# Attention and a feed-forward block in one kernel: the weights' place in SBUF, modulo 256 bytes, against the activations'

## The chip, the cores and the metric

The kernel runs on one core of a Trainium2 chip. The metric is the device time of one execution in microseconds. Before the change three runs took 956.99, 957.62 and 958.03 us; the median is 957.62.

## What is computed

Attention output of eight batches and eight heads (a downsampled full attention plus a local one within three positions), laid out as 4608 tokens of 512 values, goes through a feed-forward block:

```python
out_d = sm_attn(q_d, k_d, v_d)            # on means over 4 positions
out_up = np.repeat(out_d, factor, axis=2)
mask = np.abs(pos[:, None] - pos[None, :]) < factor
out_local = np.matmul(attn, v)            # softmax of the masked scores
x = (out_up + out_local)                  # (B, H, S, D) -> (4608, 512)
h = x @ w_in                              # 512 -> 2048
r = np.maximum(h, 0.0)
g = s * (r * r) + b
return g @ w_out                          # 2048 -> 512
```

Each float32 operand of the feed-forward block is split into a high and a low part of type float32r, and a product is three matmuls: high by high, high by low, low by high.

## The kernel before

The 4608 tokens are 18 blocks `t` of 256, the 2048 columns of the hidden layer are eight pairs `p` of two 128-column tiles (the "f pairs"). For each block and pair there is

- a first GEMM (`products1`, L617): 24 matmuls of 256 columns. The stationary operand is a 128x128 piece of `wi[p]`, the moving one a 128x256 piece of `xh` or `xl`. A block and pair's 24 matmuls are called a run here. There are 18 x 8 = 144 runs, 3,456 matmuls;
- on ACT relu, square and the cast to `gh` (`upper`, L630 to L632), on DVE the remainder `gl` (`lower`, L637);
- a second GEMM (`products2`, L691 to L693): 12 matmuls of 512 columns, 1,728 in all. Here a 128x128 piece of `gh` or `gl` is stationary and `wo[p]` is the moving operand.

While one matmul streams its moving operand, the next one's stationary operand is loaded; the page lists these loads as PEld.

Blocks 0 and 1 go through pairs 0 to 6 together while the weights arrive, then block 2, then block after block with pairs 0 to 7. Attention of later batches runs on DVE, POOL and ACT beside the GEMMs up to about 720 us; its own matmuls stand between those of the GEMMs. A plan written by hand (`PLAN`) fixes the order of the start on every engine, and a scheduler orders the rest by priorities.

Memory is laid out pool by pool in the order in which pools are opened, a tile after the other within a pool. Sizes are rounded up to 32 bytes a partition. Nearly all of it is in use: the last buffer ends at 229,320 bytes of a partition. The pools that matter here:

- `cst`: constants, the strip mask among them (L159, 384 bytes, read only at the start by L176 and L177), `eps`, `sb_s`, `sb_b` with one value each
- `one`: tiles with one buffer. `wi` and `wo` of all eight pairs stand in it (8,192 bytes each: 2 parts x 4 x 256 or 2 x 2 x 512 values), the tags `os` and `xl2` (4,096 bytes each), and attention's tiles. Tags `wi0` to `wo7` are also lent out before the weights arrive: as staging of raw weights (`load_w`, L227) and as room for the first batch's attention (`make_room`, L113)
- `two`: tiles with two buffers, among them `xh`, `xl`, `gh`, `gl`, and `pv`, which serves the weight conversion (`convert`, L240) and later local attention

Block 2's parts of x are kept in `os` and `xl2`. From block 3 on every third pair (`p % 3 == 2`, that is 2 and 5) has its g in `xl2`, under the name `gb`.

By the built program's memory map, the start addresses modulo 256 before the change are:

| tiles | modulo 256 |
|---|---|
| wi, wo of pairs 0 and 1 | 224 |
| wi, wo of pairs 2 to 7 | 96 |
| xh, xl, gh, gl | 32 |
| os, xl2 (block 2's x, and gb) | 96 |

The pieces inside a tile that a matmul takes lie multiples of 512 bytes apart, so each matmul has the distance of its two tiles. The functions that the change touches:

Of the kernel before, what the change touches and what calls it, by code (L numbers as in the profile page):

```python
# [11 lines left out]
F32 = mybir.dt.float32  # L12
F32R = mybir.dt.float32r
I32 = mybir.dt.int32
# [5 lines left out]
P = 128  # L20
# [4 lines left out]
DM = H * D  # L25
# [13 lines left out]
NFP = DFF // 256  # L39
NK = DM // P  # L40
# [9 lines left out]
STAGE = (7, 6, 7, 6, 7, 6, 7)  # L50
# [36 lines left out]
def attention_ffn_kernel(ctx, tc, qk, vw_in, vr_in, vdm, qkn, vn, w_in, w_out, s_in, b_in, out):  # L87
    nc = tc.nc
    PS = bass.MemoryType.PSUM

    cst = ctx.enter_context(tc.tile_pool(name="cst", bufs=1))
    one = ctx.enter_context(tc.tile_pool(name="one", bufs=1))
    two = ctx.enter_context(tc.tile_pool(name="two", bufs=2))
    ps = ctx.enter_context(tc.tile_pool(name="ps", bufs=1, space=PS))
# [7 lines left out]
    def take(flat, at, shape):  # L102

        v = flat[0 : shape[0], at : at + math.prod(shape[1:])]
        return v.rearrange("p (a c) -> p a c", a=shape[1]) if len(shape) == 3 else v


    def flat(tag, n, pool=one):
        return pool.tile([P, n], F32, tag=tag, name="flat")
# [1 line left out]
    room = {}  # L111

    def make_room(i):  # L113
        sc, dg = flat(f"wi{6 - i}", 2048), flat(f"wo{6 - i}", 2048)
        if i == 1:
            big = flat("x", HP * S, two)
            lp = {"vw": take(big, 0, [P, NG, P]), "vd": take(big, 768, [KM, FAC, P])}
            pl, at = big, 1280
        else:
            big = flat("wi2" if i == 2 else "wo2", 2048)  # L120
            pl, at = flat("os" if i == 2 else "xl2", 1024), 512
            lp = {"qk": take(big, 0, [P, 2, SP]), "vw": take(big, 2 * SP, [P, NG, P]),
                  "vd": take(pl, 0, [KM, FAC, P])}
        lp["vr"] = take(sc, 1792, [P, FAC, D])
        return {"sc": sc, "dg": dg, "load": lp, "pl": take(pl, at, [P, 2 * NG, 32]),
                "sm": take(pl, at + 384, [P, 2, 2 * NG])}

    def load_parts(b, hp, parts):
        if b == 0 and hp and hp not in room:
            room[hp] = make_room(hp)  # L130
        own = room[hp]["load"] if b == 0 and hp else {}
        got = ld.setdefault((b, hp), {})
        for tag in parts:
            shape, src, pool = {
                "qk": ([P, 2, SP], qk[b, hp], two),
                "vr": ([P, FAC, D], vr_in[b, hp], one),
                "vd": ([KM, FAC, P], vdm[b, hp], one),
                "vw": ([P, NG, P], vw_in[min(HP * b + hp, EU - 1)], one)}[tag]
            t = own[tag] if tag in own else pool.tile(shape, F32, tag=tag, name="t" + tag)
            nc.sync.dma_start(t, src)  # L140
            got[tag] = t
# [14 lines left out]

    mask = cst.tile([P, 3, 32], F32, name="mask")  # L159
    nc.gpsimd.memset(mask, 0.0)  # L160

    def keep(ap, pattern, base, cm):
# [31 lines left out]
    ones = cst.tile([P, P], F32, name="ones")  # L194
    nc.gpsimd.memset(ones, 1.0)
    bias = cst.tile([P, DM], F32, name="bias")
    eps = cst.tile([P, 1], F32, name="eps")
    nc.gpsimd.memset(eps, 4e-9)

    db = one.tile([P, 2 * NG, P], F32, tag="big", name="db")  # L200
# [21 lines left out]
    wi, wo, wst = {}, {}, {}  # L222
# [4 lines left out]
    def load_w(p, op):  # L227
        if op == "i":
            src = src_i[:, :, 512 * p : 512 * p + 512]
        else:  # L230
            src = src_o[:, 2 * p : 2 * p + 2]
        if p < len(STAGE):
            st = one.tile([P, 1024, 2], I32, tag=f"w{op}{STAGE[p]}", name="wst")
        else:
            st = new_x(2).rearrange("p h s -> p (h s)")[:, 0:2048].bitcast(I32)
            st = st.rearrange("p (f t) -> p f t", t=2)
        nc.sync.dma_start(st.rearrange("p (k f) t -> p k (f t)", k=src.shape[1]), src)
        wst[(p, op)] = st

    def convert(st, hi, lo, op, p):  # L240


        n = hi.shape[1]
        top, low = st[:, :, 1], st[:, :, 0]
        if n <= 512:
            f = two.tile([P, n], F32, tag="pv", name="es")
        else:
            f = one.tile([P, n], F32, tag="xl2" if op == "i" else "os", name="es")
        w = f.bitcast(I32)


        nc.scalar.mul(f, top.bitcast(F32), 2.0 ** -112)
        yield
        nc.vector.tensor_scalar(f, f, W_MAX, -W_MAX, ALU.min, ALU.max)
        nc.vector.tensor_scalar(w, w, 3, 0x7FFFFFF8, ALU.logical_shift_left, ALU.bitwise_and)
        yield
        nc.vector.scalar_tensor_tensor(w, low, 29, w, ALU.logical_shift_right, ALU.bitwise_or)  # L257
        nc.vector.scalar_tensor_tensor(w, top, -0x80000000, w, ALU.bitwise_and, ALU.bitwise_or)
        yield
        nc.scalar.copy(hi, f)  # L260
        yield
        nc.vector.tensor_tensor(lo, f, hi.bitcast(F32), ALU.subtract)  # L262

    def split_parts(p):
        wi[p] = one.tile([P, 2, NK, 256], F32R, tag=f"wi{p}", name="wi")
        wo[p] = one.tile([P, 2, 2, DM], F32R, tag=f"wo{p}", name="wo")
        for op, w in (("i", wi[p]), ("o", wo[p])):
            fl = w.rearrange("p s k f -> p s (k f)")
            n = 1024 if WIDE <= p < len(STAGE) else 512
            for j in range(0, 1024, n):  # L270
                js = slice(j, j + n)
                yield convert(wst[p, op][:, js], fl[:, 0, js], fl[:, 1, js], op, p)
# [4 lines left out]
    def new_x(b):  # L277
        if b not in xt:
            xt[b] = two.tile([P, HP, S], F32, tag="x", name="x")
        return xt[b]  # L280
# [494 lines left out]
    for op in "io":  # L775
        load_w(0, op)
    for hp in range(1, HP):
        load_parts(0, hp, ("vw",))
    sb_s = cst.tile([P, 1], F32, name="sb_s")
    nc.sync.dma_start(sb_s, bass.AP(s_in.tensor, s_in.offset, [[0, P], [1, 1]]))  # L780
    sb_b = cst.tile([P, 1], F32, name="sb_b")
    nc.sync.dma_start(sb_b, bass.AP(b_in.tensor, b_in.offset, [[0, P], [1, 1]]))
    for op in "io":
        load_w(1, op)
# [14 lines left out]

    bk = {0: banks(*range(8)), 1: two_banks(5, 6), 2: two_banks(2, 3)}  # L800
    chunks = (chunk for p in range(NFP) for chunk in split_parts(p))

    streams = {"x": begin_x(), "y": third_x(), "z": fourth_x(), "b": add_rows()}
# [15 lines left out]
    def load(name):  # L819
        if name[0] == "w":  # L820
            load_w(int(name[1]), name[2])
        else:
            load_parts(*units[int(name[1:-1])], {"k": ("qk",), "v": ("vr", "vd"), "w": ("vw",)}[name[-1]])
# [75 lines left out]
    for st in range(begin, len(order)):  # L899
        t, p = order[st]  # L900
# [73 lines left out]
```

## Time and profile before

| what | value |
|---|---|
| median of three runs | 957.62 us |
| profiled execution, device time | 957.84 us |
| its span, first to last instruction | 956.0 us |
| TensorE matmuls busy | 928.4 us |
| first GEMM (L617), busy over all 3,456 | 437.00 us |
| mean granted TensorE clock | 0.989 |

Times are microseconds unless marked ns. PE is TensorE's matmuls, PEld its weight loads, DVE is VectorE, ACT ScalarE, POOL GpSimd. A line with "xN | busy, mean ns" is a group of N instructions. Matmuls are pipelined, so the mean length of one matmul's record (280 ns for 256 columns) is longer than the distance between the starts of two neighbours; where a text speaks of spacing, it is the distance between starts. The chain of waits lists in order of time what was last at each moment: a row has the start, the length, and how many instructions in a row it covers.

### The profile page before, as it was taken

How to read it: one execution, taken by the hardware profiler on the slowest of the kernel's cores; microseconds unless marked ns; L12 is line 12 of the kernel's file. 1: busy time of each engine (PE TensorE's matmuls, PEld its weight loads, DVE VectorE, ACT ScalarE, POOL GpSimd, SP SyncE). 2: the span in 40 equal slices, each digit the busy share in tenths (PEclk: the TensorE clock that was granted, in tenths of full speed). 3: DMA queues.
4: the chain of work that ended last, by engine and by line, in shares of the span. 5: the costliest groups of instructions: out<-in, count | busy, mean ns of one | idle time of the engine just before them, and what ended most of it. 6: DMA issues, size and time to landing. Idle time of an engine off the chain costs nothing.

```text
span 956.0 us, 18449 instructions
## 1 busy us (share of the span) xinstructions
PE 928.4 (97%) x7316; PEld 835.7 (87%) x7316; DVE 639.5 (67%) x1134; ACT 476.8 (50%) x1133; POOL 416.2 (44%) x440
## 2 busy tenths in 40 slices
PE   6699999999999999999999999999999999999998
PEld 5588888888898999998899999999899999999986
DVE  8999999845587788787868787887777321112021
ACT  7977774466552636344454544454544333333231
POOL 6401130010577676867776868676776200000000
PEclk9699999999999999999999999999999999999999
DMA  9755413123232323323232323232311000000000
GB/s 322 268 167 183 143 46 118 63 75 100 87 117 89 117 90 110 95 80 108 88 116 80 126 80 126 81 126 79 114 55 44 1 23 2 23 1 23 1 23 22
DMA packets 31750, 86.25 MB, mean 90 GB/s; under 512 B 3248, under 2 KB 7856, under 8 KB 31664
## 3 DMA queue, kind: packets, MB, share of 16 engines
q1 hardware_dynamic: 31664, 85.08, 26.9%
q8 instruction: 57, 0.93, 0.4%
q14 instruction: 29, 0.24, 0.1%
HBM read 75.63 MB, written 9.44 MB: 89 GB/s over the span
## 4 chain that ended last, share of the span: by engine, by line
PE 84%; DVE 7%; DMA 3%; POOL 2%; ACT 1%; issue 1%; SPq 0%; DVEq 0%; POOLq 0%
PE ph L617 38%; PE po L691 13%; PE po L692 13%; PE po L693 12%; PE sa L327 2%; PE ol L464 1%; PE up L368 1%; POOL pr L522 1%; DMA tqk<-in_qk_dram 1%; PE ot L554 1%; DMA wst<-in_moe_w_in_dram 1%; DMA tvd<-in_vdm_dram 1%; PE up L366 1%; PE sl L421 1%; DVE es L257 1%
## 5 line engine op out<-in xcount | busy, mean ns | idle before, releaser
L617 PE MATMUL ph<-xh,wi 128*128 128x256 f32 x2176 | 406.7, 280 | 1.5 <-DVE gl L637 1.5
L617 PEld LDWEIGHTS ph<-xh,wi 128*128 128x128 f32 x2176 | 342.0, 189 | 7.3 <-DVE gl L637 1.9
L617 PE MATMUL ph<-xl,wi 128*128 128x256 f32 x1152 | 323.4, 281 | 0.0
L522 POOL TENSOR_TENSOR pr<-lqk 128x576 f32<-128x576 f32 x140 | 201.3, 1461 | 77.7 <-DMA lqk<-in_qkn_dram 47.7
L617 PEld LDWEIGHTS ph<-xl,wi 128*128 128x128 f32 x1152 | 217.3, 189 | 4.5
L630 ACT ACTIVATE ph<-ph 128x512 f32<-128x512 f32 x144 | 83.7, 582 | 248.1 <-PE ph L617 239.4
L691 PE MATMUL po<-wo,gh 128*128 128x512 f32 x456 | 181.8, 399 | 2.0 <-DVE os L669 1.7
L693 PE MATMUL po<-wo,gl 128*128 128x512 f32 x456 | 179.1, 394 | 1.1 <-DVE gl L637 1.0
L692 PE MATMUL po<-wo,gh 128*128 128x512 f32 x456 | 180.2, 395 | 0.0
L637 DVE TENSOR_TENSOR gl<-ph,gh 128x512 fp32r<-128x512 f32 x114 | 77.9, 684 | 125.0 <-ACT gh L632 124.7
L544 POOL TENSOR_TENSOR acc<-acc,pv 128x576 f32<-128x576 f32 x80 | 121.0, 1512 | 48.8 <-DVE acc L544 25.9
L524 DVE TENSOR_REDUCE st<-pr 128x9 f32<-128x576 f32 x140 | 105.9, 757 | 31.7 <-POOL pr L522 28.2
L693 PEld LDWEIGHTS po<-wo,gl 128*128 128x128 f32 x456 | 85.7, 188 | 20.5 <-DVE gl L637 2.5
L691 PEld LDWEIGHTS po<-wo,gh 128*128 128x128 f32 x456 | 85.7, 188 | 18.7 <-DVE os L669 2.1
L632 ACT CAST gh<-ph 128x512 fp32r<-128x512 f32 x114 | 66.6, 586 | 66.4 <-PE po L692 61.1
L692 PEld LDWEIGHTS po<-wo,gh 128*128 128x128 f32 x456 | 85.8, 188 | 15.7 <-DVE wo L262 0.3
L297 POOL TENSOR_TENSOR dq<-vt 80x64 f32<-80x64 f32 x58 | 22.6, 401 | 174.5 <-PE up L368 172.9
L543 DVE TENSOR_TENSOR pv<-lv,st 128x576 f32<-128x576 f32 x120 | 86.9, 747 | 14.2 <-POOL acc L544 13.6
L631 ACT ACTIVATE ph<-ph 128x512 f32<-128x512 f32 x144 | 83.8, 583 | 3.5
L692 PE MATMUL po<-wo,gb 128*128 128x512 f32 x120 | 47.8, 398 | 0.0
L691 PE MATMUL po<-wo,gb 128*128 128x512 f32 x120 | 47.1, 392 | 0.0
L693 PE MATMUL po<-wo,gb 128*128 128x512 f32 x120 | 46.8, 392 | 0.0
(158 smaller groups left out, 1167.5 us busy)
## 6 DMA issues: line engine op xcount, KB each, us to landing
tqk<-in_qk_dram SPq DMA_DIRECT2D x30, 584.0 KB, 3.9
lqk<-in_qkn_dram SPq DMA_DIRECT2D x20, 768.0 KB, 4.6
lv<-in_vn_dram SPq DMA_DIRECT2D x20, 480.0 KB, 3.4
out_dram<-os SPq DMA_DIRECT2D x17, 512.0 KB, 3.0
wst<-in_moe_w_in_dram SPq DMA_DIRECT2D x7, 1024.0 KB, 6.2
wst<-in_moe_w_out_dram SPq DMA_DIRECT2D x7, 1024.0 KB, 5.0
tvd<-in_vdm_dram SPq DMA_DIRECT2D x29, 160.0 KB, 2.6
tvr<-in_vr_dram SPq DMA_DIRECT2D x29, 128.0 KB, 3.1
```

Source lines behind the costliest of these rows:

```text
L522: nc.gpsimd.tensor_tensor(pr, lqk[:, 0:CH], lqk[:, CH + o : 2 * CH + o], ALU.mult)
L524: nc.vector.tensor_reduce(ls[:, :, o], pr, AX.X, ALU.add)
L543: nc.vector.tensor_tensor(pv, lv[:, o : o + CH], w, ALU.mult)
L544: (nc.vector if o % 3 == 1 else nc.gpsimd).tensor_tensor(acc[:, :, h], acc[:, :, h], pv, ALU.add)
L617: nc.tensor.matmul(ph[:, j], wi[p][:, s, k, f], xk[:, k], start=k == 0 and s == 0 and xk is xh, stop=k == NK - 1 and s == 1)
L630: nc.scalar.activation(ph, ph, AF.Relu)
L631: nc.scalar.activation(ph, ph, AF.Square)
L632: nc.scalar.copy(gh, ph)
L637: nc.vector.tensor_tensor(gl, acc.pop((t, p)), gh.bitcast(F32), ALU.subtract)
L691: nc.tensor.matmul(po[m], gh[:, j, ms], wo[p][:, 0, j], start=first, stop=False)
L692: nc.tensor.matmul(po[m], gh[:, j, ms], wo[p][:, 1, j], start=False, stop=False)
L693: nc.tensor.matmul(po[m], gl[:, j, ms], wo[p][:, 0, j], start=False, stop=last)
```

## The change

The weights of pairs 0-1, 2-3, 4-5 and 6-7 move out of `one` into four pools of their own. Each of the four begins with a gap of 64 bytes; a further pool with a gap of 32 bytes stands behind them. The strip mask moves from `cst` into a buffer of `pv`, and `eps`, `sb_s` and `sb_b` become three columns of one tile; both make room for the gaps.

```diff
     cst = ctx.enter_context(tc.tile_pool(name="cst", bufs=1))
+    weights = []
+    for i in range(NFP // 2):
+        weights.append(ctx.enter_context(tc.tile_pool(name=f"w{i}", bufs=1)))
+        weights[i].tile([P, 16], F32, tag="gap", name="gap")
+    ctx.enter_context(tc.tile_pool(name="gap", bufs=1)).tile([P, 8], F32, name="gap")
+    wpool = lambda tag: weights[int(tag[2]) // 2]
     one = ctx.enter_context(tc.tile_pool(name="one", bufs=1))
...
-        sc, dg = flat(f"wi{6 - i}", 2048), flat(f"wo{6 - i}", 2048)
+        sc, dg = (flat(f"w{op}{6 - i}", 2048, weights[3 - (i + 1) // 2]) for op in "io")
...
-            big = flat("wi2" if i == 2 else "wo2", 2048)
+            big = flat("wi2" if i == 2 else "wo2", 2048, weights[1])
...
-    mask = cst.tile([P, 3, 32], F32, name="mask")
+    mask = two.tile([P, 3, 32], F32, tag="pv", name="mask")
...
-    eps = cst.tile([P, 1], F32, name="eps")
+    small = cst.tile([P, 3], F32, name="small")
+    eps, sb_s, sb_b = (small[:, i : i + 1] for i in range(3))
...
-            st = one.tile([P, 1024, 2], I32, tag=f"w{op}{STAGE[p]}", name="wst")
+            tag = f"w{op}{STAGE[p]}"
+            st = wpool(tag).tile([P, 1024, 2], I32, tag=tag, name="wst")
...
-        wi[p] = one.tile([P, 2, NK, 256], F32R, tag=f"wi{p}", name="wi")
-        wo[p] = one.tile([P, 2, 2, DM], F32R, tag=f"wo{p}", name="wo")
+        wi[p] = wpool(f"wi{p}").tile([P, 2, NK, 256], F32R, tag=f"wi{p}", name="wi")
+        wo[p] = wpool(f"wo{p}").tile([P, 2, 2, DM], F32R, tag=f"wo{p}", name="wo")
...
-    sb_s = cst.tile([P, 1], F32, name="sb_s")
     nc.sync.dma_start(sb_s, bass.AP(s_in.tensor, s_in.offset, [[0, P], [1, 1]]))
-    sb_b = cst.tile([P, 1], F32, name="sb_b")
     nc.sync.dma_start(sb_b, bass.AP(b_in.tensor, b_in.offset, [[0, P], [1, 1]]))
```

By the memory map of the changed program:

| tiles | modulo 256 | weights minus x, first GEMM | g minus weights, second GEMM |
|---|---|---|---|
| wi, wo of pairs 0 and 1 | 224 | 96 | 160 |
| wi, wo of pairs 2 and 3 | 32 | 160 | 96 (pair 2 from gb: 160) |
| wi, wo of pairs 4 and 5 | 96 | 224 | 32 (pair 5 from gb: 96) |
| wi, wo of pairs 6 and 7 | 160 | 32 | 224 |
| xh, xl, gh, gl | 128 | | |
| os, xl2 | 192 | | |

On all five engines the instructions stand in the same order as before, and so do the DMA issues. One wait is new. On ACT, in the start, before (a row's name of several tiles is written as `flat`, the first batch's borrowed room; `es` is the conversion's tile in `pv`):

```order
L342 ACTIVATE pd<-pd,dsm 96x144 x2
L331 ACTIVATE flat<-flat 96x3 [waits DVE_49]
L333 ACTIVATE flat<-sa,flat 96x144 [waits PE_49,Activation_49]
L333 ACTIVATE flat<-sa,flat 96x144 x2
L252 ACTIVATE es<-wst 128x512
L331 ACTIVATE flat<-flat 96x3 [waits DVE_49]
```

And after, where the file's lines stand eight further down (L260 is L252 before):

```order
L350 ACTIVATE pd<-pd,dsm 96x144 x2
L339 ACTIVATE flat<-flat 96x3 [waits DVE_49]
L341 ACTIVATE flat<-sa,flat 96x144 [waits PE_49,Activation_49]
L341 ACTIVATE flat<-sa,flat 96x144 x2
L260 ACTIVATE es<-wst 128x512 [waits Pool_49]
L339 ACTIVATE flat<-flat 96x3 [waits DVE_49]
```

The order is the same; the second conversion step now waits for POOL, which wrote the mask into the buffer that this step takes.

## The prediction

> **What bounds the kernel now.** I read the page first, then the chain of waits for one late output block, the timeline inside single runs, and the groups of windows that hold one weight pair each.
>
> ```profile
> PE 928.4 (97%) x7316; PEld 835.7 (87%) x7316; DVE 639.5 (67%) x1134; ACT 476.8 (50%) x1133; POOL 416.2 (44%) x440
> PEclk9699999999999999999999999999999999999999
> PE 84%; DVE 7%; DMA 3%; POOL 2%; ACT 1%; issue 1%; SPq 0%; DVEq 0%; POOLq 0%
> PE ph L617 38%; PE po L691 13%; PE po L692 13%; PE po L693 12%; PE sa L327 2%; PE ol L464 1%; PE up L368 1%; POOL pr L522 1%; DMA tqk<-in_qk_dram 1%; PE ot L554 1%; DMA wst<-in_moe_w_in_dram 1%; DMA tvd<-in_vdm_dram 1%; PE up L366 1%; PE sl L421 1%; DVE es L257 1%
> L617 PE MATMUL ph<-xh,wi 128*128 128x256 f32 x2176 | 406.7, 280 | 1.5 <-DVE gl L637 1.5
> ```
>
> TensorE is busy 97% of the span at a full granted clock after the start, and 38 + 13 + 13 + 12 = 76% of the chain that ended last is the two GEMMs. So the time is the number of matmuls, which the change leaves alone, times the spacing of two neighbours. That spacing can be read per weight pair. The chain of waits in block 16 (854 to 907 us, no attention left on the other engines) shows the eight runs of 24 first-GEMM matmuls, pairs 0 to 7 in order:
>
> ```profile
> 854.69 2.83 PE ph L617 x24
> 860.28 2.83 PE ph L617 x24
> 868.60 2.75 PE ph L617 x24
> 873.44 2.73 PE ph L617 x24
> 876.86 2.73 PE ph L617 x24
> 883.08 2.74 PE ph L617 x24
> 887.88 2.83 PE ph L617 x24
> 893.47 2.83 PE ph L617 x24
> ```
>
> The runs have the same instructions, shapes and x; what differs between them is where the pair's weights lie. Pairs 2 to 5 take 2.73 to 2.75 us (113.8 ns a matmul), pairs 0, 1, 6 and 7 take 2.83 us (117.9 ns). In the program's memory map x's parts lie at 32 modulo 256; wi and wo of pairs 0 and 1 at 224, of all others at 96. So w minus x is 192 for pairs 0 and 1 (slow) and 64 for the rest (fast, or slow for 6 and 7). Block 2 has its x in other tiles ("os" and "xl2", at 96), which gives two more distances. For pair 2 (distance 0):
>
> ```profile
> 168.36 2.87 PE ph L617 x24
> ...
> 179.41 1.44 PE ph L617 x12
> ```
>
> That is 2.87 us, and 1.44 x 2 = 2.88 us for 24; I use 2.875 (119.8 ns). For pairs 0 and 1 (distance 128) the timeline has the low part's matmuls, every third one, the first and the sixteenth of sixteen:
>
> ```profile
> 150.66 0.28 PE L617 MATMUL ph<-xl,wi 128*128 128x256 f32 x1
> ...
> 156.00 0.28 PE L617 MATMUL ph<-xl,wi 128*128 128x256 f32 x1
> ```
>
> 45 matmuls lie between these starts: 5.34 / 45 = 118.7 ns, 2.848 us for 24. So all four multiples of 64 are on show, and 64, which most pairs have now, is the best: 2.875 at 0, (2.75 + 2.73 + 2.73 + 2.74 + 2.83 + 2.83) / 6 = 2.768 at 64, 2.848 at 128, 2.83 at 192.
>
> Is it the other engines? The stretch windows of block 9 and block 16 (DVE 40.5 against 7.7 us, POOL 37.6 against 0) speak against it:
>
> ```profile
> 519.00:568.00 49.00, 49.00 (x333) 44.76 (x333) 40.49 (x72) 23.88 (x63) 37.60 (x35) 1.00 0.30 99
> 854.00:898.00 44.00, 44.00 (x288) 39.96 (x288) 7.68 (x11) 14.01 (x24) 0.00 (x0) 1.00 0.03 13
> ```
>
> The first run of block 9 in the chain, with all that beside it, is as long as pair 0's in block 16:
>
> ```profile
> 519.46 2.83 PE ph L617 x24
> ```
>
> **The change part by part.** No instruction is added, removed or moved on any engine, and no DMA. Three things change: addresses, one shared buffer, one shared scalar tile.
>
> *Shared mask.* The mask takes one of the two "pv" buffers, and the second conversion step on ACT (L252) now waits for POOL. What it waits for and when it runs in the trace of before:
>
> ```profile
> 6.79 0.30 POOL L163 TENSOR_SCALAR_AFFINE_SELECT mask<-mask 32x32 f32<-32x32 f32 x1
> 7.13 0.20 DVE L177 CAST maskb<-mask 128x64 bf16<-128x64 f32 x1
> 21.79 0.71 ACT L252 ACTIVATE es<-wst 128x512 f32<-128x512 f32 x1
> ```
>
> The mask is last touched at 7.33 us and its buffer is next written at 21.79 us. The wait is over 14 us before ACT comes to it: 0, and if that cover were gone, what stands behind it on ACT would shift by at most the overlap. The scalar tile ("small") is written by the same memset and the same two DMAs and read by the same instructions: 0.
>
> *First GEMM.* After the change x's parts lie at 128 modulo 256 and the pools at 224, 32, 96 and 160: distances 96, 160, 224 and 32 for pairs 0-1, 2-3, 4-5, 6-7 (block 2, x at 192: 32, 96, 160, 224). None of these stands in the trace; all are odd multiples of 32, and every distance measured is a multiple of 64. The nearest rows are the two neighbours on either side, so I take their mean: 32 gets (2.875 + 2.768) / 2 = 2.822, 96 gets 2.808, 160 gets 2.839, 224 gets 2.853; mean 2.830 us a run. Now: (2 x 2.83 + 6 x 2.768) / 8 = 2.784 for 136 runs and (2 x 2.848 + 6 x 2.875) / 8 = 2.868 for block 2's eight: 401.5 us. Then: 144 x 2.830 = 407.6. Term: **+6.1 us**. Bounds: all runs as pairs 3 and 4 (2.73): 393.1, so -8.4; all as distance 0 (2.875): 414.0, so +12.5.
>
> *Second GEMM.* Here wo is the moving operand and g the stationary one, so I count g minus wo. Windows that hold one pair each, in the order pair 1 (distance 64), pair 4 (192), pair 5 (0, its g lies in "gb"), pair 7 (192):
>
> ```profile
> L693 PE MATMUL po<-wo,gl 128*128 128x512 f32 x4 | 1.6, 395 | 0.0
> L691 PE MATMUL po<-wo,gh 128*128 128x512 f32 x4 | 1.6, 394 | 0.0
> L692 PE MATMUL po<-wo,gh 128*128 128x512 f32 x4 | 1.6, 394 | 0.0
> ...
> L691 PE MATMUL po<-wo,gh 128*128 128x512 f32 x4 | 1.6, 394 | 0.0
> L692 PE MATMUL po<-wo,gh 128*128 128x512 f32 x4 | 1.6, 394 | 0.0
> L693 PE MATMUL po<-wo,gl 128*128 128x512 f32 x4 | 1.6, 392 | 0.0
> ...
> L691 PE MATMUL po<-wo,gb 128*128 128x512 f32 x4 | 1.6, 393 | 0.0
> L692 PE MATMUL po<-wo,gb 128*128 128x512 f32 x4 | 1.6, 390 | 0.0
> L693 PE MATMUL po<-wo,gb 128*128 128x512 f32 x3 | 1.2, 392 | 0.0
> ...
> L693 PE MATMUL po<-wo,gl 128*128 128x512 f32 x4 | 1.6, 394 | 0.0
> L692 PE MATMUL po<-wo,gh 128*128 128x512 f32 x4 | 1.6, 392 | 0.0
> L691 PE MATMUL po<-wo,gh 128*128 128x512 f32 x4 | 1.6, 388 | 0.0
> ```
>
> Means: 394.3 at 64, (393.3 + 391.3) / 2 = 392.3 at 192, 391.7 at 0; for 128 I take the mean of these, 392.8. By pairs, before: two at 64, two at 0 (2 and 5), four at 192: 392.65. After: pairs 0, 1, 2 at 160, 3 and 5 at 96, 4 at 32, 6 and 7 at 224, priced by neighbours 392.6, 393.6, 393.0, 392.0: 392.75. Term: 0.1 ns x 1,728 = **+0.2 us**. Bounds: all at the best row (388): -4.65 x 1,728 = -8.0 us; all at the worst (394.3): +1.65 x 1,728 = +2.9 us.
>
> *Other engines* also get new addresses. Nothing in the trace prices that; since TensorE is the bound, 0.
>
> Sum: +6.3 us on the profiled execution's 957.84 (its span is 956.0, 1.84 lie around it) gives 964.1; the median of the three runs is 0.22 lower, 963.9. I say **964.0 us**. All of it counts at the end, since nearly every run is itself a piece of the chain.
>
> **The rivals.** *Odd multiples of 32 are free of it (faster).* If half a step of 64 keeps the two reads apart, every run falls to the length of pairs 3 and 4 and every second-GEMM matmul to its best row: at most -8.4 - 8.0 = -16.4 us. The first matmuls of a run cost more even in fast pairs (pair 2's 2.75 against 2.73), so I take three quarters, -12: 945.6. For it: a spacing at one distance can be either (pairs 6 and 7 against 2 to 5), so the cause is fine-grained, and a shift of 32 is finer than anything tried. Against it: three of four known distances are slow, and nothing marks 32 as special.
>
> *A wash.* One or two pools find a fast spacing, the others lose theirs. With two pools at 2.73 and two at 2.83, 144 x 2.78 = 400.3, -1.2 us: 956.4, or with the second GEMM's spread of some 2 us about 954 to 960. For it: the four pools sample four distances, as now two are mixed.
>
> *The address does not matter.* Then the change does nothing: 957.6. Against it: the pairs differ by 0.1 us a run in the same order of work, and for pair 0 from block 9 to block 16 alike. The Trainium skill, SBUF — State Buffer, "Who interferes with whom", gives TensorE two independent read ports for the moving operand and for weight loads and says that it never waits on anyone; by that rule the sum would be 0. The rows above disagree with it: 113.8 against 117.9 ns for equal matmuls.
>
> *Slower at the far end.* The same mechanism as my forecast, decided by how many pools land on a distance like 0: all four give +12.5 + 2.9 = +15.4, 973.
>
> **How the numbers follow.** Forecast mechanism (no offset better than its neighbours, far end included) 0.50; odd multiples free 0.30; wash 0.15; address without effect 0.05. What a measurement of this kernel tells from no change is about 0.2%, 1.9 us. The wash goes half to faster, half to no change. Faster 0.30 + 0.08 = 0.38; same 0.05 + 0.07 = 0.12; slower 0.50. The range reaches from the faster rival's 944 to near the far end, 972; the forecast's own range is 960 to 972.
>
> **What would show it.** In the chain of waits of block 16 the eight runs should read about 2.81, 2.81, 2.84, 2.84, 2.85, 2.85, 2.82, 2.82 instead of four at 2.74. If pairs 0 and 1 and two more come at 2.73, it is the wash; if all do, the faster rival. Runs that keep their lengths by pair mean that it was not the address. A wait of ACT before L252 near 21.8 us would show the shared mask wrong. A run under 2.72 us, shorter than any in this trace, would break the whole scale of prices.

## The result, and the profile after

The changed kernel takes 967.30 us (median of four runs, 966.63 to 967.56) against 957.83 us for the kernel before on the same chip (median of four runs, the three above and one more): 1.0105 times as long, 95% interval 1.009 to 1.012. The profiled execution has a span of 965.5 us, 9.5 more than before. The forecast was 964.0, slower, in a range of 944 to 972.

From the page of the kernel after, the engine line and the largest groups of the two GEMMs (lines stand eight further down: L625 is L617 before, L699 to L701 are L691 to L693):

```profile
PE 940.3 (97%) x7316; PEld 843.6 (87%) x7316; DVE 637.9 (66%) x1134; ACT 476.9 (49%) x1133; POOL 414.8 (43%) x440
L625 PE MATMUL ph<-xh,wi 128*128 128x256 f32 x2176 | 414.1, 283 | 0.0
L699 PE MATMUL po<-wo,gh 128*128 128x512 f32 x456 | 182.8, 401 | 1.4 <-DVE os L677 1.3
L700 PE MATMUL po<-wo,gh 128*128 128x512 f32 x456 | 180.9, 397 | 0.0
L701 PE MATMUL po<-wo,gl 128*128 128x512 f32 x456 | 180.0, 396 | 0.7 <-DVE gl L645 0.6
L700 PE MATMUL po<-wo,gb 128*128 128x512 f32 x120 | 48.3, 403 | 0.0
```

The same four second-GEMM groups on the page of the kernel before:

```profile
L691 PE MATMUL po<-wo,gh 128*128 128x512 f32 x456 | 181.8, 399 | 2.0 <-DVE os L669 1.7
L692 PE MATMUL po<-wo,gh 128*128 128x512 f32 x456 | 180.2, 395 | 0.0
L693 PE MATMUL po<-wo,gl 128*128 128x512 f32 x456 | 179.1, 394 | 1.1 <-DVE gl L637 1.0
L692 PE MATMUL po<-wo,gb 128*128 128x512 f32 x120 | 47.8, 398 | 0.0
```

TensorE is busy 11.9 us longer with the same 7,316 matmuls, while DVE, ACT and POOL hardly move: the matmuls themselves got longer, 283 instead of 280 ns in the first GEMM, 396 to 401 instead of 394 to 399 in the second, 403 instead of 398 in the group that reads gb. How much that makes in all is read from a window over the whole span with the first GEMM's line alone, before and then after (window, length, busy time of the matmuls and of the weight loads with their counts, granted clock, DMA share and GB/s):

```profile
0.00:956.00 956.00, 437.00 (x3456) 422.77 (x3456) 0.99 0.27 90
```

```profile
0.00:965.50 965.50, 444.15 (x3456) 429.32 (x3456) 1.00 0.27 89
```

That is 7.15 us for the first GEMM. The granted clock does not explain it: it reads 0.99 in the window before and 1.00 in the one after. To compare kernels below I use two sums, taken from the start times of all matmuls in the trace: S1 adds up, over neighbouring first-GEMM matmuls, the distance of their starts minus 113.33 ns; S2 does the same for the second GEMM with 226.67 ns. These are the shortest spacings that hold over a whole run in any kernel here, and distances over 135 and 250 ns are left out as waits. Before, S1 is 8.3 us and S2 5.6; after, 15.5 and 10.3. So +7.2 and +4.7 us, 11.9 in all, of which 9.5 reach the end. Of the other 2.4, 1.6 are waits between these matmuls, which got shorter; the last 0.8 I did not trace.

The chain of waits for block 16 after, the same eight runs, pairs 0 to 7:

```profile
862.57 2.83 PE ph L625 x24
868.20 2.82 PE ph L625 x24
876.63 2.87 PE ph L625 x24
881.61 2.88 PE ph L625 x24
885.19 2.80 PE ph L625 x24
891.48 2.80 PE ph L625 x24
896.38 2.84 PE ph L625 x24
902.02 2.84 PE ph L625 x24
```

The four runs of 2.73 to 2.75 us that stood at pairs 2 to 5 are gone, and none has come elsewhere. And the new wait on ACT, in the timeline:

```profile
21.23 0.66 ACT L260 ACTIVATE es<-wst 128x512 f32<-128x512 f32 x1
```

L260 begins 0.09 us after the instruction before it on ACT (an accumulator read at 21.14), as it did before: the shared mask costs nothing there.

### The profile page after: what moved, and what is told of

Read it like the earlier page. It is cut to its first block, busy times and chain, and to the rows that moved or that the text cites. A ratio compares the mean times of both kernels' runs of the same rounds, so it can differ in the third digit from the quotient of the medians.

```text
span 965.5 us, 18449 instructions
## 1 busy us (share of the span) xinstructions
PE 940.3 (97%) x7316; PEld 843.6 (87%) x7316; DVE 637.9 (66%) x1134; ACT 476.9 (49%) x1133; POOL 414.8 (43%) x440
## 4 chain that ended last, share of the span: by engine, by line
PE 85%; DVE 7%; POOL 3%; ACT 2%; DMA 1%; issue 1%; DVEq 0%; POOLq 0%; ACTq 0%
PE ph L625 38%; PE po L699 13%; PE po L701 13%; PE po L700 13%; PE sa L335 2%; POOL pr L530 2%; PE up L376 1%; PE ot L562 1%; PE ol L472 1%; DVE es L266 1%; DVE es L265 1%; PE sl L429 1%; PE up L374 1%; PE tr L363 1%; DMA x<-in_moe_w_in_dram 1%
## 5 line engine op out<-in xcount | busy, mean ns | idle before, releaser
L625 PE MATMUL ph<-xh,wi 128*128 128x256 f32 x2176 | 414.1, 283 | 0.0
L625 PEld LDWEIGHTS ph<-xh,wi 128*128 128x128 f32 x2176 | 344.2, 189 | 5.4
L625 PE MATMUL ph<-xl,wi 128*128 128x256 f32 x1152 | 325.7, 283 | 0.0
L625 PEld LDWEIGHTS ph<-xl,wi 128*128 128x128 f32 x1152 | 217.5, 189 | 4.7
L699 PE MATMUL po<-wo,gh 128*128 128x512 f32 x456 | 182.8, 401 | 1.4 <-DVE os L677 1.3
L701 PE MATMUL po<-wo,gl 128*128 128x512 f32 x456 | 180.0, 396 | 0.7 <-DVE gl L645 0.6
L701 PEld LDWEIGHTS po<-wo,gl 128*128 128x128 f32 x456 | 85.7, 188 | 21.1 <-DVE gl L645 1.8
L699 PEld LDWEIGHTS po<-wo,gh 128*128 128x128 f32 x456 | 85.8, 188 | 19.0 <-DVE os L677 1.7
L551 DVE TENSOR_TENSOR pv<-lv,st 128x576 f32<-128x576 f32 x120 | 86.9, 747 | 10.7 <-POOL acc L552 10.3
L699 PE MATMUL po<-wo,gb 128*128 128x512 f32 x120 | 47.6, 397 | 0.0
L701 PE MATMUL po<-wo,gb 128*128 128x512 f32 x120 | 47.3, 396 | 0.0
```

The source lines that it names most:

```text
L551: nc.vector.tensor_tensor(pv, lv[:, o : o + CH], w, ALU.mult)
L625: nc.tensor.matmul(ph[:, j], wi[p][:, s, k, f], xk[:, k], start=k == 0 and s == 0 and xk is xh, stop=k == NK - 1 and s == 1)
L699: nc.tensor.matmul(po[m], gh[:, j, ms], wo[p][:, 0, j], start=first, stop=False)
L701: nc.tensor.matmul(po[m], gl[:, j, ms], wo[p][:, 0, j], start=False, stop=last)
```

## The experiments

Times are medians; "ratio" is to the kernel before, measured beside it on the same chip, with its 95% interval. Where "one run" stands, there is only one time; beside the two sweeps the kernel before took 955.83 us, beside the low half at 96 it took 956.88. Three explanations are tested first. Theory A: the distance of the two operands modulo 256 sets the spacing. Rival B: what counts is whether weights and activations lie at the same place modulo 64. Rival C: the shared mask and scalar tile, or the new places of other tiles, cost the time. "Distance" is weights minus x for the first GEMM and g minus weights for the second, modulo 256 bytes.

| kernel | time, us | ratio | S1, us | S2, us |
|---|---|---|---|---|
| after | 967.30 | 1.0105 [1.009, 1.012] | 15.5 | 10.3 |
| mask alone | 956.82 | 1.0003 [0.9994, 1.0012] | 8.4 | 5.6 |
| x and g 32 further | 963.55 | 1.0072 [1.0055, 1.0089] | 14.0 | 6.6 |
| g alone 32 further | 965.79 | 1.0088 [1.0072, 1.0105] | 15.9 | 7.4 |
| x alone 32 further | 964.86 | 1.0078 [1.0063, 1.0093] | 12.9 | 9.5 |
| no gaps | 956.88 | 1.0000 [0.9991, 1.0010] | 9.1 | 4.8 |
| no gaps, rear 256 further | 957.80 | 1.0009 [0.9999, 1.0018] | 8.9 | 4.7 |
| no gaps, all 32 further | 956.63 | 0.9995 [0.9985, 1.0004] | 8.8 | 4.7 |
| g at 0 | 956.05 | 0.9986 [0.9977, 0.9995] | 11.6 | 1.5 |
| gl at 64 | 956.99 | 0.9997 [0.9988, 1.0006] | 6.9 | 5.7 |
| sweep in steps of 32 | 961.96 | one run | 15.5 | 3.4 |
| sweep, 16 off | 962.88 | one run | 17.5 | 3.2 |
| low half at 96 | 959.30 | one run | 10.4 | 5.0 |

### The mask alone

The kernel before with the mask in `pv` and the three scalars in one tile; filler tiles hold every other address.

```diff
-    mask = cst.tile([P, 3, 32], F32, name="mask")
+    cst.tile([P, 96], F32, name="fill")
+    mask = two.tile([P, 3, 32], F32, tag="pv", name="mask")
...
+    small = cst.tile([P, 3], F32, name="small")
+    eps, sb_s, sb_b = (small[:, i : i + 1] for i in range(3))
+    cst.tile([P, 16], F32, name="fill2")
```

> The kernel before with the shared mask buffer and the shared scalar tile alone; filler tiles keep every other address as it was. Theory A and rival B: as before, 957.8 +- 1 us. Rival C: 962 us or more.

It takes 956.82 us against 956.71 for before. This half of the change is free, as predicted, and rival C falls. S1 and S2 are those of before within 0.1 us, so two programs with the same addresses repeat each other.

### x and g 32 bytes further on

```diff
-    ctx.enter_context(tc.tile_pool(name="gap", bufs=1)).tile([P, 8], F32, name="gap")
+    ctx.enter_context(tc.tile_pool(name="gap", bufs=1)).tile([P, 16], F32, name="gap")
```

> The kernel after, with x's and g's parts (and os, xl2) 32 bytes further on; weights stay. Distances weights minus x become 64, 128, 192 and 0 for pairs 0-1, 2-3, 4-5, 6-7, all multiples of 64 as before the change, but dealt to other pairs. Theory A (the distance modulo 256 sets the spacing, whichever pair has it): in block 16 the runs of 24 read 2.73 to 2.83 us for pairs 0-1, 2.85 for 2-3, 2.83 for 4-5, 2.88 for 6-7; the second GEMM falls back to about 4 ns a matmul over 226.7; total 961 to 966 us. Rival B (not the distance but the half: all is well when weights and activations lie at the same place modulo 64, here 32 both): every pair as in before, total 957 +- 2 us. Rival C (the shared mask and scalar tile or the other tiles' new places cost it): total 967 us as after.

963.55 us, as theory A had it. The chain in block 16, pairs 0 to 7:

```profile
859.75 2.73 PE ph L625 x24
865.28 2.72 PE ph L625 x24
873.48 2.89 PE ph L625 x24
878.44 2.84 PE ph L625 x24
881.98 2.83 PE ph L625 x24
888.30 2.72 PE ph L625 x24
893.09 2.87 PE ph L625 x24
898.75 2.87 PE ph L625 x24
```

The runs at the short spacing have gone from pairs 2 to 5 to pairs 0 and 1, the ones that now stand at 64; the pairs at 0 take 2.87 us as block 2 did before. So the spacing goes with the distance and not with the pair. Rival B falls: all tiles lie alike modulo 64 here, and five of the eight pairs do not have the short spacing. One row nobody had expected: pair 5, at 192, reads 2.72 us where pair 4, at 192 too, reads 2.83. So 64 is not the only distance with two spacings. Pairs 2 and 3, both at 128, differ as well (2.89 and 2.84).

### Each GEMM's part alone

`g alone` puts gh and gl behind a gap of their own; `x alone` does it on top of the edit above, with a gap of 8 words in place of 24, so that gh and gl fall back to where they were.

```diff
+    ctx.enter_context(tc.tile_pool(name="gap", bufs=1)).tile([P, 24], F32, name="gap")
+    gpool = ctx.enter_context(tc.tile_pool(name="gparts", bufs=2))
...
-        gh = two.tile([P, 2, TB], F32R, tag="gh", name="gh")
-        gl = two.tile([P, 2, TB], F32R, tag="gl", name="gl")
+        gh = gpool.tile([P, 2, TB], F32R, tag="gh", name="gh")
+        gl = gpool.tile([P, 2, TB], F32R, tag="gl", name="gl")
```

> The kernel after with gh and gl alone 32 bytes further on: g minus weights becomes 192 (pairs 0, 1), 128 (3), 64 (4), 0 (6, 7), pairs 2 and 5 keep 160 and 96 since their g lies elsewhere; weights minus x keep the odd multiples of 32. Theory A: the first GEMM's sum over 113.3 stays at 15 to 16 us, the second's over 226.7 falls from 10.3 to about 8 us; total 963 to 965.5 us. If only one of the two GEMMs cared, the time would be as after, 966.5, or the second GEMM would fall to 5 us and the time to 961.

> The kernel after with x's parts (and os, xl2) alone 32 bytes further on, gh and gl where they were: weights minus x 64, 128, 192, 0 by pairs; g minus weights keeps 160, 96, 32, 224, but pairs 2 and 5, whose g lies in xl2, get 192 and 128. Theory A: the first GEMM's sum over 113.3 is that of the kernel with x and g 32 further, 13 to 15 us, the second's 9 to 10 us; total 964 to 967 us.

With g alone moved, S1 stays (15.9 against 15.5) and S2 falls from 10.3 to 7.4. The time is 965.79, just over the expected 963 to 965.5, though S1 + S2 is 23.3 us where 23 to 24 was expected: the rest of the span is 0.9 us longer than in the kernel after. With x alone moved, S2 stays near (9.5; pairs 2 and 5 read their g from xl2, which moved too) and S1 falls to 12.9, just under the expected 13 to 15; 964.86. Each GEMM answers mainly to its own distance, and the two parts nearly add up: 2.9 us for g and 2.6 for x by the sums, 5.2 with both moved. Mainly, not alone: with the same first-GEMM distances S1 is 12.9 with x alone and 14.0 with x and g moved.

### All pairs at 64, and three places for the same distances

No gaps puts all weights at one distance, 64 in the first and 192 in the second GEMM. Two more kernels keep these distances modulo 256: one moves all behind the weights by 256, one moves weights and all behind them by 32.

```diff
-        weights[i].tile([P, 16], F32, tag="gap", name="gap")
-    ctx.enter_context(tc.tile_pool(name="gap", bufs=1)).tile([P, 8], F32, name="gap")
```

> The kernel after without any gap: all sixteen weight tiles at 160 modulo 256 (and 160 modulo 512), x's and g's parts at 96 (352 modulo 512), so every pair has weights minus x = 64 modulo 256 (320 modulo 512, as pairs 2 to 5 had before), g minus weights 192 (0 for pairs 2 and 5 from gb). Theory A modulo 256: all pairs as the mean of pairs 2 to 7 before (1.9 ns over 113.3 a matmul), total 954 to 957 us. Theory A modulo 512: all pairs as 2 to 5 before, runs of 2.73 to 2.75 us for every pair in block 16, total about 953.5 us. Rival B: 957. Rival C: 967.

> As the kernel without gaps, but x, g and all tiles behind the weights 256 bytes further on: the same distance modulo 256, but weights minus x = 64 modulo 512 for every pair, as pairs 6 and 7 had before. Theory A modulo 256: the same time as without gaps, within 1 us, and the same runs. Theory A modulo 512: every pair as 6 and 7 before, runs of 2.83 us in block 16, total 957 to 959 us, 3 to 5 us over the kernel without gaps. Rivals B and C: no difference between the two.

> The kernel without gaps, with everything from the scalar tile on 32 bytes further: weights at 192, x and g at 128 modulo 256, all now multiples of 64, and the same distances (64, and 192 or 0 in the second GEMM). Theory A (only the distance between the two operands counts): the same runs in block 16 as without gaps (pairs 4 and 5 2.73 us, the others 2.83) and the same time within 1 us. Rival B (each tile's own place modulo 64 counts): other runs, 2 us or more either way.

Pairs 3 to 5 in the chain of block 16, no gaps:

```profile
872.95 2.83 PE ph L623 x24
876.48 2.73 PE ph L623 x24
882.65 2.73 PE ph L623 x24
```

The same with the rear 256 further on:

```profile
873.55 2.83 PE ph L624 x24
877.08 2.73 PE ph L624 x24
883.25 2.73 PE ph L624 x24
```

And with all 32 further on:

```profile
872.28 2.83 PE ph L624 x24
875.80 2.73 PE ph L624 x24
881.97 2.73 PE ph L624 x24
```

All eight runs agree between the three kernels, pairs 4 and 5 at 2.73 and the rest at 2.83. So at these distances the place itself does not count: not the distance modulo 512, which I had held possible since pairs 6 and 7 differ from 2 to 5 by 256, and not the place modulo 64. But the expected gain of no gaps, 954 to 957 by theory A, came out at the upper end, 956.88: at one and the same distance of 64, six of eight pairs hold the long spacing here. The distance allows the short one; something else decides whether a run gets it. The second GEMM is no different: at its one distance of 192 the pairs' mean spacings in blocks 14 to 17 lie 2.2 to 5.3 ns over 226.67.

### What decides at 64: g at 0, and gl at 64

g at 0 is no gaps with gh and gl moved to the weights' own place modulo 256 (the edit of g alone with 32 words). In gl at 64, whose edit is shown, gl alone stands another 64 bytes on.

```diff
+    hpool = ctx.enter_context(tc.tile_pool(name="ghigh", bufs=2))
+    hpool.tile([P, 2, TB], F32R, tag="gh", name="gh0")
+    ctx.enter_context(tc.tile_pool(name="gap2", bufs=1)).tile([P, 16], F32, name="gap2")
+    lpool = ctx.enter_context(tc.tile_pool(name="glow", bufs=2))
...
-        gh = two.tile([P, 2, TB], F32R, tag="gh", name="gh")
+        gh = hpool.tile([P, 2, TB], F32R, tag="gh", name="gh")
-        gl = two.tile([P, 2, TB], F32R, tag="gl", name="gl")
+        gl = lpool.tile([P, 2, TB], F32R, tag="gl", name="gl")
```

> The kernel without gaps, with gh and gl moved so that g minus weights is 0 modulo 256 for every pair instead of 192; x keeps its distance 64. In the runs so far a second-GEMM matmul at 0 took 0.6 to 3.3 ns over 226.7, at 192 2.2 to 4.9. Theory A: the second GEMM's sum over 226.7 falls from 4.8 to 1 to 4 us, the first GEMM's stays between 3 and 9 us, since which of the two spacings at 64 a run takes may change; total 951 to 957 us. Rival B: no change from the kernel without gaps.

> The kernel with g at distance 0, but gl another 64 bytes on: gh minus wo stays 0, gl minus wo is 64 (pairs 2 and 5, from gb, stay at 0); weights minus x stay 64. Theory D (at 64 a run holds one of two spacings, and which one depends on how the second GEMM before it ends; after an undisturbed one at 226.7 it is always the slow one): with one second-GEMM matmul in three disturbed, the runs after it fall into 2.73 us in block 16 at least for half of the pairs; second GEMM 2 to 4 ns over 226.7; total 952 to 957 us. Rival E (the slow spacing there comes from g's tiles standing at another place, not from what came before): all runs stay at 2.83 us, the second GEMM gets slower, total 957 to 960 us.

With g at 0 the second GEMM is undisturbed: in the late blocks every start follows the last by 226 or 227 ns. All six of its groups in the window of block 16 (852 to 896 us) read alike; three of them:

```profile
L700 PE MATMUL po<-wo,gh 128*128 128x512 f32 x24 | 9.3, 389 | 0.0
L701 PE MATMUL po<-wo,gl 128*128 128x512 f32 x24 | 9.3, 389 | 0.0
L699 PE MATMUL po<-wo,gb 128*128 128x512 f32 x8 | 3.1, 389 | 0.0
```

S2 falls from 4.8 to 1.5 us. But S1 rises from 9.1 to 11.6, beyond the 3 to 9 that were expected, and pairs 4 and 5, at the short spacing without gaps, are now at the long one like all others, though neither x nor their weights have moved against each other:

```profile
874.64 2.83 PE ph L625 x24
880.87 2.83 PE ph L625 x24
```

With gl at 64 the second GEMM is disturbed again, and the runs of block 16 read, pairs 0 to 7:

```profile
852.68 2.74 PE ph L628 x24
858.15 2.83 PE ph L628 x24
866.52 2.74 PE ph L628 x24
871.34 2.74 PE ph L628 x24
874.77 2.74 PE ph L628 x24
880.98 2.83 PE ph L628 x24
885.84 2.83 PE ph L628 x24
891.44 2.74 PE ph L628 x24
```

Five hold the short spacing. Pairs 1, 5 and 6 hold the long one, and just these three follow matmuls of pair 5 or 2, whose g lies in gb and was not moved. Over blocks 14 to 17 of this kernel the trace has 32 runs: the 20 that follow a second GEMM whose last two matmuls took 229 or 230 and 235 or 236 ns all hold the short one (113.3 ns), the 12 that follow one ending in 226 and 227, or in 231 to 233, all the long one (117.8). With g at 0 all 32 follow an undisturbed one, and all hold the long spacing. The three kernels without gaps bear it out. There runs behind a second GEMM at the same distance of 192 hold either spacing (in block 16 pairs 0, 2, 3 and 7 the long one, pair 4 the short one), so g's place does not decide: of their 96 runs in these blocks the 69 whose last matmul before took 226 or 227 ns hold the long spacing, the 27 after 230 to 235 ns the short one. So theory D holds: at 64 a run keeps one of two spacings, and how the second GEMM before it ends goes with which. Rival E falls. One reserve: the last of these times is the distance to the run's own first start, so the end of the second GEMM and the run may have a cause in common. The gain of one GEMM is paid back by the other: S1 + S2 is 13.9 us without gaps, 13.1 with g at 0, 12.6 with gl at 64. g at 0 is the one kernel whose interval lies below 1 (0.9986, [0.9977, 0.9995]). That is 0.14%, less than the 0.2% that the prediction held for no change, and gl at 64, with the smaller sum, is at 0.9997; I do not count it as a gain.

### All distances in steps of 16

With g at 0 from every wo, each pair's wi stands 32 bytes further than the last one's; the second kernel is 16 off.

```diff
...
+        if i:
+            weights["i", i].tile([P, 8], F32, tag="gap", name="gap")
...
```

```diff
...
+        wide = wpool(f"wi{p}").tile([P, 2052], F32R, tag=f"wi{p}", name="wi")
+        wi[p] = wide[:, 4:2052].rearrange("p (s k f) -> p s k f", s=2, k=NK)
...
```

> As the kernel with g at distance 0 from all wo (there every second-GEMM matmul took 226.7 ns), but each pair's wi 32 bytes further than the last one's: weights minus x = 96, 128, 160, 192, 224, 0, 32, 64 for pairs 0 to 7. It reads the price of all eight distances in one run, all after an undisturbed second GEMM. Theory A: odd multiples of 32 as in the kernel after (96: 117.6, 160: 120, 224: 116.7, 32: 118.2 ns), 0 at 119.8, 128 at 118.7, 192 and 64 at 117.8 or 113.4. If one of them reads 113.4 here, a kernel with all pairs there should take about 948 us. If the order of pairs and not the distance set the spacing, the lengths would follow the pair as before the change.

> The same with the wi another 16 bytes off: distances 80, 112, 144, 176, 208, 240, 16, 48 for pairs 0 to 7. If the price changes smoothly with the distance, each lies between its neighbours of the sweep in steps of 32, and none is at 113.4. If a free spacing needs the two reads to be apart by something other than a multiple of 32, one or two of these read 113.4.

Block 16 in steps of 32, distances 96, 128, 160, 192, 224, 0, 32, 64:

```profile
858.30 2.84 PE ph L628 x24
863.89 2.84 PE ph L628 x24
872.21 2.88 PE ph L628 x24
877.13 2.83 PE ph L628 x24
880.66 2.81 PE ph L628 x24
886.89 2.87 PE ph L628 x24
891.85 2.84 PE ph L628 x24
897.41 2.83 PE ph L628 x24
```

The mean spacing of a first-GEMM matmul in blocks 13 to 17, by distance, from the starts in these two traces:

| distance | 0 | 16 | 32 | 48 | 64 | 80 | 96 | 112 | 128 | 144 | 160 | 176 | 192 | 208 | 224 | 240 |
|---|---|---|---|---|---|---|---|---|---|---|---|---|---|---|---|---|
| ns | 119.6 | 118.4 | 118.3 | 118.4 | 117.7 | 118.7 | 118.5 | 120.0 | 118.4 | 119.9 | 120.0 | 118.4 | 117.9 | 116.8 | 116.7 | 119.8 |

None of the twelve distances that are not multiples of 64 gets to 113.4, nor did any pair of the kernel after. Of the odd multiples of 32, three read as they did after the change, whichever pair has them; 96 reads 118.5 here and 117.5 to 117.7 there. The rival of my prediction that odd multiples are free of it is gone. The price does not change smoothly in these two kernels: 112 lies above both neighbours.

What the table cannot say: from block 14 on each distance stands behind nearly one and the same ending of the second GEMM, and 64 itself shows only its long spacing, since the last matmuls before it took 226 or 227 ns. The distances 80 and 48 stand behind such an ending too, so a short spacing there is not ruled out. And the expectation that the second GEMM would be undisturbed did not hold: every g stands at 0 from its wo as in g at 0, but S2 is 3.4 and 3.2 instead of 1.5 us. Of the distances only the first GEMM's differ, so the second GEMM too seems to answer to what runs before it.

### Which read meets which

```diff
...
+            wide = wpool("wi4").tile([P, 2, 1028], F32R, tag="wi4", name="wi")
+            flats = [wide[:, 0, 0:1024], wide[:, 1, 4:1028]]
...
```

> The kernel without gaps, but for pair 4 the low half of wi lies 32 bytes further, at distance 96 from x, its high half stays at 64 (pair 4's runs read 113.3 ns a matmul without gaps). In each group of three matmuls the stationary operands are high, high, low; all three moving ones keep their place. If a matmul's own stationary operand counts, the third of each group is the slow one; if the load of the next matmul's stationary operand counts, which runs while the current one streams, the second is. If neither, all three or none. Pair 4's run is 2.75 to 2.82 us in block 16; all other pairs as without gaps, unless what precedes them changed.

The low half of pair 4's wi lies 32 bytes further on than its high half. Pair 4's run goes from 2.73 to 2.85 us, beyond the expected 2.75 to 2.82:

```profile
877.89 2.85 PE ph L631 x24
```

By the starts in blocks 14 to 16, without a run's first group, the three matmuls of a group take about 118.0, 118.4 and 120 ns. The third is the slowest, which speaks for a matmul's own stationary operand. But the whole run has also fallen into the long spacing, against which (117.8 ns) the excess is about 0.2, 0.6 and 2.3 ns, so a stall may show at a matmul later than the one it arose in. Pair 5's run fell to 2.83 as well. I count this as inconclusive.

## Why the prediction came out

The direction and the path were right; the time came 3.3 us above the forecast. The stated range also took in the faster rival, so it is a weak test; the forecast's own 960 to 972 holds too.

- **TensorE's spacing as the bound.** Right. S1 + S2 goes up by 11.9 us, and the end by 9.5.
- **Order, mask, scalar tile: 0.** Right; the mask alone is 1.0003.
- **First GEMM, +6.1 us.** Right in size: +7.2. The neighbours' mean gave 2.81, 2.84, 2.85 and 2.82 us for pairs 0-1, 2-3, 4-5 and 6-7; block 16 has 2.83 and 2.82, 2.87 and 2.88, 2.80 and 2.80, 2.84 and 2.84. The rule behind it was only half right, and that the sum fits is in part luck: 160 came out above both of its neighbours, 0.04 us a run over its forecast, 224 below both, 0.05 under its own, and the two cancel. What was lost is the short spacing of 113.3 ns, which was seen at 64 and 192 and at none of the distances after the change.
- **Second GEMM, +0.2 us.** Wrong in size: +4.7. It is the mis-sized term: it alone is 4.5 us over its forecast. With the first GEMM's 1.1 over and 2.4 that did not reach the end, the whole came out 3.2 us over (9.5 against 6.3). The step that failed is the same mean of neighbours: I mixed 391.7, 394.3 and 392.3 ns into 392.75 for the new distances, where the means of the matmuls' records rose by 2 ns for gh and gl and 4 to 5 for gb. In spacing (blocks 13 to 17) the pairs stood 2.1 to 5.9 ns over 226.67 before and 6.0 to 8.1 after; by distance 2.5 to 5.4 before and 6.2 to 7.1 after, so all odd multiples of 32 are worse than the worst distance before. Moving g alone by 32 gave 2.9 us of it back. The premise that a distance has one price fails here too: at 192 the pairs without gaps read 2.2 to 5.3 ns over. My upper bound for the term, +2.9, was below what came.
- **The far end** (973) was decided by how many pools land on a distance like 0. One did: 160, at 2.875.
- **The wash and the free odd multiples.** Neither: four odd multiples, none at the short spacing.
- **The address does not matter.** Refuted by moving the short spacing from pair to pair with x. The Trainium skill (SBUF — State Buffer, "Who interferes with whom") gives TensorE one read port for the moving operand and an independent one for weight loads. The runs here do not agree with two reads that leave each other alone: the spacing of equal matmuls goes from 113.3 to 120.0 ns with the distance between the two operands.
- What the prediction lacked: that at 64 one distance has two spacings and what runs before goes with the choice. It had pairs 6 and 7 before its eyes and averaged them into its price for 64.

Not tried: a second GEMM that is undisturbed but for its last matmuls, which by the runs above should leave both GEMMs near their shortest; and the distances 80 and 48 behind a disturbed one. Which of TensorE's reads meet, and why modulo 256, stays open.

## What to carry to other kernels

When TensorE is the bound and its matmuls are of one shape, compare the spacing of starts between tiles that differ only in place: a few nanoseconds that go with a tile are worth a look at the memory map. A price read at some distances does not carry to those between them, so sample the new ones before moving everything there. And count what precedes: with g at 0 the second GEMM lost 3.3 us of stalls and the first one gained 2.5.

## What the runs showed of the hardware

- The spacing of float32r matmuls depends on the distance of their two operands in SBUF modulo 256 bytes, and on what runs before them. At equal distances two other places (256 bytes further behind the weights, 32 bytes further for all) gave the same eight runs. A 256-column matmul took 113.3 ns at best and 120.0 at worst, a 512-column one 226.7 and, in the mean of the worst pair, 234.8.
- At 64 there are two stable spacings, 113.3 and 117.8 ns, kept to the end of a run of 24 matmuls. Which one a run has goes with the last two matmuls before it in all 64 runs of blocks 14 to 17 in two kernels (g at 0 and gl at 64), and with the last one in all 96 of the three kernels without gaps.
- Work on the other engines did not change it: in the kernel before, pair 0's run is 2.83 us in block 9, beside full attention, and in block 16, without it.
